# Attention's products further behind their inputs, and another order of loads in the first block

## The chip, the cores and the metric

The kernel runs on one core of a Trainium2 chip. The core has a matrix engine (TensorE, PE in the rows; its weight loads are PEld), two engines for elementwise work (VectorE, DVE, and ScalarE, ACT), GpSimd (POOL) and a queue from which transfers are issued (SyncE, SP). The metric is the device time in microseconds of one execution. A row says "L369" for line 369 of the kernel.

## What is computed

Three layers in a row over 8 x 576 = 4608 tokens of 512 numbers:

```python
def _attn_ref(q, k, v, g_norm):
    kv = np.einsum('bhsd,bhse->bhde', k, v)
    out = np.einsum('bhsd,bhde->bhse', q, kv)
    rms = np.sqrt(np.mean(out * out, axis=-1, keepdims=True) + 1e-06)
    return (out / rms * g_norm).astype(np.float32)

def _moe_ref(x, w_in, w_out):            # 512 -> 2048 -> 512
    h = x @ w_in
    pos, neg = h >= 1.0, h <= -1.0
    g = np.where(pos, h, np.where(neg, 0.0, (h + 1.0) ** 2 / 4.0))
    return (g @ w_out).astype(np.float32)

def _moe2_ref(x, expert_emb, tau, w1, w2):   # 8 experts, 512 -> 1024 -> 512
    ...
    expert_idx = np.argmax(xn @ en.T / tau, axis=1)
    for e in range(E):
        mask = expert_idx == e
        h = np.maximum(x[mask] @ w1[e], 0.0)
        out[mask] = gate_w[mask, None] * (h @ w2[e])
    return out
```

w_in and w_out of the second layer come as 64-bit floats; everything else is 32 bits wide.

## The kernel before

**Tiling.** The tokens are 36 tiles of 128, and three tiles make a block, so the dense layer runs over 12 blocks. K and V come in batches of 576 rows, five pieces each (`kv_loads`, L260); `kv_task` (L278) multiplies the pieces into a PSUM bank `kvp` and copies its diagonal to `kvd`. `att_task` (L312) handles one tile of tokens: it loads q (`qt`, one buffer), multiplies it with `kvd` (L336), squares on ScalarE (L351), sums on VectorE (L354), takes the root on ScalarE (L238, in `rsqrt`) and its inverse on VectorE, scales the tile (L358, `xk`), transposes it on TensorE (L369, four products into the bank `xp`), and writes the transposed tile in two parts, rounded (L385, ScalarE) and rest (L387, VectorE), to `xT`, of which there are two buffers, one for each block. `dense` (L1005) goes through 16 chunks of a block: 12 products `h <- xT, ra` (L1025), a gate (`gate_task`, L953), and two chunks later 9 products `acc <- rb, g` (L1048). Weights and activations are split into two rounded parts, so each product is made of three passes. After a block, `evac_task` (L515) empties the three `acc` banks into `row` buffers, and `route_task` (L550) picks the expert of each token and scatters the rows. Beside all that, `exp_task` (L475) splits the experts' weights and writes them back to memory for the third layer, which starts at some 945 us.

**The first block.** It has no weights yet. `w_task` (L404) loads one raw tile of 512 KB (`raw`, four buffers), makes a 32-bit float of each 64-bit one with a copy on ScalarE (L420) and three operations on VectorE (L429, L433, L437), then splits it (L443 on ScalarE, L192 on GpSimd). There are 32 such tiles, w_in's (i0 to i15) and w_out's (o0 to o15), in the order i0, i1, i2, i3, o0, i4, o1, i5 and so on. `warm` (L988) multiplies zeros until the first block's three tiles are there.

**Order.** Nothing is scheduled by the hardware beyond each engine's own queue, which runs in program order. The order of each queue is made by a planner in the kernel itself, `Flow` (L71): each task is a generator that yields the engine it needs next and an estimated cost; `run` (L132) takes, among all tasks, the step that could start first by the planner's clocks, and among steps of one engine within 0.05 us the one of the smallest priority number. Transfers are put at `dma` (L113): one after another at 360 KB per us, 1.65 us on top. Setting `f.now` forward between two steps delays, in the plan, the next step of that task; the instruction itself then waits only for what its data need. `SLACK = 0.7` is such a distance: L363 puts the transposes 0.7 us behind the scaling. `yield "ev"` waits for an event of the plan, `yield "get"` for a buffer.

Constants come by six transfers (`small_loads`, L216): the identity and one row of weights as `cs`, then `gcol`, `R`, `pcol`, `taub`, `tris`; a seventh, `ce`, comes ahead of the third layer (L1071). `AHEAD = 1` raw tile has a priority ahead of the first K and V (L1136).

Of the kernel before, what the change touches and what calls it, by code (L numbers as in the profile page):

```python
# [7 lines left out]
F32 = mybir.dt.float32  # L8
F32R = mybir.dt.float32r
BF16 = mybir.dt.bfloat16  # L10
I32 = mybir.dt.int32
U32 = mybir.dt.uint32
AF = mybir.ActivationFunctionType
# [5 lines left out]
P = 128  # L19
# [5 lines left out]
NE = 8  # L25
# [9 lines left out]
SLACK = 0.7  # L35
AHEAD = 1
AGAIN = 0.13
# [3 lines left out]

K_W8, K_BASE, K_PAR, K_E, K_MORE, K_P, K_END = 128, 136, 144, 152, 160, 168, 169


def consts(cap):

    import ml_dtypes
    import numpy as np

    c = np.zeros((P, K_END), np.float32)  # L50
    e = np.arange(NE)
    c[:, :P] = np.eye(P)
    c[:, K_W8 : K_W8 + NE] = NE - e
    c[:, K_BASE : K_BASE + NE] = e * cap
    c[:, K_PAR : K_PAR + NE] = e % 2
    c[:, K_E : K_E + NE] = e
    c[:, K_MORE : K_MORE + NE] = e < NE - 1
    c[:, K_P] = np.arange(P)
    tri = np.concatenate([np.triu(np.ones((P, P)), 1), np.ones((P, P))], 1).astype(ml_dtypes.bfloat16)
    return c, tri  # L60

# [9 lines left out]
class Flow:  # L71
# [6 lines left out]
    def __init__(self):  # L78
        self.tasks = []
        self.clock = {}  # L80
        self.pool = {}
        self.events = {}
        self.now = 0.0
        self.dmas = 0.0
        self.count = 0

# [26 lines left out]
    def dma(self, size):  # L113

        self.dmas = max(self.dmas, self.now + 0.65) + size / 360e3
        return self.dmas + 1.0

    def resolve(self):
# [34 lines left out]
@with_exitstack  # L153
def tile_kernel(ctx: ExitStack, tc: tile.TileContext, qT, k, v, g2, w_in, w_out, emb, tau, w1, w2, cst, tri, out):
    nc = tc.nc
# [26 lines left out]
    f = Flow()  # L182
# [11 lines left out]
    def rows_dma(out_, in_, size, wait=True):  # L194
        nc.sync.dma_start(out=out_, in_=in_)
        done = f.dma(size)
        if wait:
            f.now = done
        return done

    KB = 1024.0
# [14 lines left out]
    def small_loads():  # L216
        yield "sp", 0.45
        cs = consts_["cs"] = keep.tile([P, K_W8 + NE], F32, name="cs")
        f.set("cs", rows_dma(cs, cst[:, 0 : K_W8 + NE], 70 * KB, False))
        for name, src, n, dt in (  # L220
            ("gcol", g2, 1, F32), ("R", cst[:, K_BASE : K_BASE + NE], NE, F32), ("pcol", cst[:, K_P : K_P + 1], 1, F32),
            ("taub", tau.partition_broadcast(P), 1, F32), ("tris", tri, 2 * P, BF16),
        ):
            yield "sp", 0.45
            consts_[name] = late.tile([P, n], dt, name=name)
            done = rows_dma(consts_[name], src, 8 * KB, False)
        f.set("small", done)
        yield "pool", 0.1
        for name, val in (("neg1", -1.0), ("half", 0.5)):
            consts_[name] = late.tile([P, 1], F32, name=name)  # L230
            nc.gpsimd.memset(consts_[name], val)

    def rsqrt(pool, a, n, nm, bufs=1):
# [26 lines left out]
    def kv_loads(start, end):  # L260

        if start == 0:
            for name in ("xT", "xT"):
                yield "get", name
        else:
            yield "ev", ("kvt", start - 1)
        for u in range(start, end):
# [10 lines left out]
    def kv_task(b):  # L278
        kvp = None
        for j in range(NKV):  # L280
# [4 lines left out]
            kt, vt, n, done = kv_tiles.pop(u)  # L285
            f.now = max(f.now, done)
            yield "pe", 0.5
# [16 lines left out]
        for h in range(2):  # L304
            r = slice(h * D, h * D + D)
            nc.scalar.activation(out=kvd[b % 2][r, :, r], in_=kvp[r, :, r], func=AF.Copy)
        f.put("kvp")
        f.set(("kv", b))

    xT = {}  # L310

    def att_task(i, otag="op", xtag="op"):  # L312
# [9 lines left out]
        else:  # L322
            qt = sr.tile([P, DM], F32, name="qt", tag="qt", bufs=1)
        rows_dma(qt, qT[i], 256 * KB)
        b0, b1 = (i * P) // S, (i * P + P - 1) // S
        yield "ev", ("kv", b0)
# [35 lines left out]
        f.put(otag)  # L362
        f.now += SLACK  # L363
        yield "ev", "cs"
# [283 lines left out]
    def first_expert():  # L648

        ce = ord_["ce"]  # L650
        col = lambda c0: ce[:, c0 - K_BASE : c0 - K_BASE + NE]
        c = new("fc")
# [410 lines left out]
    def start_slots():  # L1063
# [6 lines left out]
        pools["x"] = ctx.enter_context(tc.tile_pool(name="m2x", bufs=1, side="right", reuse_waits="tile"))  # L1070
        ce = ord_["ce"] = late.tile([P, K_END - K_BASE], F32, name="ce")  # L1071
        rows_dma(ce, cst[:, K_BASE:K_END], 16 * KB)
        yield "pool", 0.7
# [49 lines left out]
    def chained(*gens):  # L1123
        for g_ in gens:
            yield from g_

    f.add(kv_loads(0, NKV), 0)
    f.add(kv_task(0), 0)
# [103 lines left out]
def lay_out(inputs):  # L1232
# [9 lines left out]
    w_in = np.ascontiguousarray(w_in.transpose(2, 1, 0, 3)).reshape(NF, P, 512)  # L1242
    g2 = np.concatenate([inputs["g_norm"], inputs["g_norm"]]).reshape(P, 1)
    cst, tri = consts(tok + P)
    def turned(a):
# [4 lines left out]
    return {  # L1250
        "qT": qT, "k": flat(inputs["k"]), "v": flat(inputs["v"]), "g2": np.ascontiguousarray(g2), "w_in": bits(w_in),
        "w_out": bits(np.ascontiguousarray(inputs["moe_w_out"])), "emb": inputs["moe2_expert_emb"],
        "tau": np.asarray(inputs["moe2_tau"]).reshape(1), "w1": turned(inputs["moe2_w1"]), "w2": inputs["moe2_w2"],
        "cst": cst, "tri": tri,
    }
# [18 lines left out]
```

## Time and profile before

| | us |
|---|---|
| median of 3 runs | 1448.8 |
| lowest, highest | 1446.64, 1449.76 |
| the profiled execution | 1447.99 |
| its span, first to last instruction | 1446.2 |
| PE busy in the span | 1391.8 |
| DVE busy in the span | 1120.5 |

The span is what the rows count in, from its first instruction on. A busy share is a mean over stages that have different limits, so the stages have to be read one by one. Idle time of an engine is told with what ended it; only idle time of the engine that sets the pace of a stage costs time. The granted clock (PEclk) is TensorE's, as a share of full speed.

### The profile page before, as it was taken

What the parts mean: (1) busy time and instruction counts of PE and PEld (TensorE: products, weight loads), DVE (VectorE), ACT (ScalarE), POOL (GpSimd) and SP (SyncE); (2) the same over time, 40 slices, a digit from 0 to 9 for tenths busy, and PEclk for the clock granted to TensorE, in tenths of its full rate; (3) what the DMA queues carried; (4) which work ended last, traced back from release to release, by engine and by line L of the source; (5) the groups of instructions that cost most, each with busy time, mean ns of one, the idle gap of its engine ahead of it and who ended that gap; (6) DMA issues with size and microseconds to landing.
All of it is one profiled execution on the core that took longest, in us unless ns stands there. A gap on an engine that the chain in (4) does not pass through costs nothing. (4 is left out here: it accounts for less than half of the span.)

```text
span 1446.2 us, 24714 instructions
## 1 busy us (share of the span) xinstructions
PE 1391.8 (96%) x7474; PEld 1194.2 (83%) x7474; DVE 1120.5 (77%) x2629; ACT 618.5 (43%) x1259; POOL 377.0 (26%) x347
## 2 busy tenths in 40 slices
PE   6889999999999999999999999999999999999995
PEld 5768889889889888888889999878888888888884
DVE  5888989696969797978778756485887778888883
ACT  4766455545555554555555534332222222222221
POOL 1675233323233332333332332310000010000000
PEclk9999999999999999999999999999999999999998
DMA  9764654555655564545454200583111137774175
GB/s 290 240 223 169 204 193 166 190 196 183 216 191 177 176 232 170 180 167 180 164 181 162 69 31 1 222 334 112 53 46 45 46 136 278 273 288 178 46 298 207
DMA packets 85456, 249.99 MB, mean 173 GB/s; under 512 B 10190, under 2 KB 10446, under 8 KB 80592
## 3 DMA queue, kind: packets, MB, share of 16 engines
q1 hardware_dynamic: 79168, 229.21, 44.9%
q0 software_dynamic: 6160, 19.18, 3.4%
q8 instruction: 68, 1.11, 0.3%
q14 instruction: 60, 0.49, 0.1%
HBM read 423.87 MB, written 90.02 MB: 355 GB/s over the span
## 5 line engine op out<-in xcount | busy, mean ns | idle before, releaser
L1048 PE MATMUL acc<-rb,g 128*128 128x512 f32 x1728 | 448.5, 400 | 9.9 <-POOL rb L192 6.4
L1025 PE MATMUL h<-xT,ra 128*128 128x384 f32 x2304 | 441.3, 338 | 0.6 <-DVE xT L387 0.4
L1025 PEld LDWEIGHTS h<-xT,ra 128*128 128x128 f32 x2304 | 403.3, 188 | 17.6 <-DVE xT L387 0.6
L1048 PEld LDWEIGHTS acc<-rb,g 128*128 128x128 f32 x1728 | 319.8, 189 | 72.1 <-POOL rb L192 8.8
L897 DVE STREAM_TRANSPOSE ht<-h 32x256 f32<-32x256 f32 x592 | 264.1, 446 | 55.1 <-PE h L822 44.2
L192 POOL TENSOR_TENSOR sp<-sp 128x512 fp32r<-128x512 f32 x128 | 182.3, 1429 | 441.3 <-ACT sp L466 421.8
L561 DVE CUSTOM_DVE_ANT_0 tr<-row,en 128x512 bf16<-128x512 f32 x288 | 228.0, 796 | 3.0 <-ACT row L526 0.3
L822 PE MATMUL y<-rb,hT 128*128 x888 | 217.9, 401 | 5.1 <-DMA rb<-ws 5.1
L822 PE MATMUL h<-ra,xT 128*128 x888 | 213.9, 396 | 0.0
L822 PEld LDWEIGHTS y<-rb,hT 128*128 128x128 f32 x888 | 165.2, 189 | 43.3 <-issue 6.0
L822 PEld LDWEIGHTS h<-ra,xT 128*128 128x128 f32 x888 | 167.1, 188 | 40.4
L964 ACT ACTIVATE h<-h,neg 128x384 f32<-128x384 f32 x176 | 97.6, 554 | 214.8 <-DVE cl L957 214.8
L975 DVE TENSOR_TENSOR cl<-h,cl 128x384 f32<-128x384 f32 x176 | 97.4, 554 | 65.7 <-ACT cl L968 65.5
L980 ACT ACTIVATE g<-cl 128x384 fp32r<-128x384 f32 x192 | 100.7, 525 | 110.2 <-DVE cl L975 70.6
L957 DVE TENSOR_SCALAR cl<-h 128x384 f32<-128x384 f32 x192 | 105.8, 551 | 45.9 <-PE h L1025 44.9
L192 DVE TENSOR_TENSOR g<-cl,g 128x384 fp32r<-128x384 f32 x144 | 100.6, 698 | 31.9 <-ACT g L980 30.4
L968 ACT ACTIVATE cl<-cl,half 128x384 f32<-128x384 f32 x192 | 116.6, 607 | 0.0
L912 ACT ACTIVATE hT<-ht 128x512 fp32r<-128x512 f32 x74 | 46.2, 624 | 160.4 <-DVE ht L897 160.4
L941 POOL DMA_INDIRECT out<-ys,xr x24 | 23.4, 974 | 269.0 <-ACT ys L938 241.7
L778 ACT ACTIVATE xT<-xp 128x512 fp32r<-128x512 f32 x42 | 25.1, 598 | 159.3 <-PE xp L771 159.2
L466 ACT ACTIVATE sp<-sp 128x512 fp32r<-128x512 f32 x128 | 79.2, 622 | 12.6 <-DMA sp<-in_w 11.2
L192 POOL TENSOR_TENSOR g<-cl,g 128x384 fp32r<-128x384 f32 x48 | 53.4, 1113 | 88.8 <-ACT g L980 85.9
(156 smaller groups left out, 1079.2 us busy)
## 6 DMA issues: line engine op xcount, KB each, us to landing
ra<-ws SPq DMA_DIRECT2D x78, 2048.0 KB
rb<-ws SPq DMA_DIRECT2D x76, 2048.0 KB
ws<-sp SPq DMA_DIRECT2D x128, 512.0 KB
sp<-in_w SPq DMA_DIRECT2D x128, 256.0 KB
qt<-in_qT SPq DMA_DIRECT2D x33, 256.0 KB
raw<-in_w_in SPq DMA_DIRECT2D x16, 512.0 KB
raw<-in_w_out SPq DMA_DIRECT2D x16, 512.0 KB
kt<-in_k SPq DMA_DIRECT2D x26, 256.0 KB
```

Of the source, the lines that this page charges most:

```text
L192: eng.tensor_tensor(out=out_, in0=a, in1=hi.bitcast(F32), op=ALU.subtract)
L466: nc.scalar.activation(out=sp[:, 0], in_=r, func=AF.Copy)
L561: nc.vector.tensor_tensor_reduce(out=trash("tr", e % 2), in0=rows[blk, t][:, 0:DM], in1=en[:, e], scale=1.0, scalar=0.0, op0=ALU.mult, op1 ...
L822: m = nc.tensor.matmul(out=out, lhsT=lhsT, rhs=ring[:, bass.ds(pars[t], 1), c0 : c0 + 512].rearrange("p a f -> p (a f)"), start=start, sto ...
L897: nc.vector.transpose(out=ht[t][s, :, r], in_=h[r, 256 * q : 256 * q + 256].rearrange("p (c a) -> p c a", c=8))
L957: nc.vector.tensor_scalar(out=cl, in0=h, scalar1=-1.0, scalar2=1.0, op0=ALU.max, op1=ALU.min)
L964: nc.scalar.activation(out=over, in_=h, func=AF.Relu, bias=consts_["neg1"])
L968: nc.scalar.activation(out=cl, in_=cl, func=AF.Square, bias=consts_["half"], scale=0.5)
L975: nc.vector.tensor_tensor(out=cl, in0=over, in1=cl, op=ALU.add)
L980: nc.scalar.activation(out=g[:, 0], in_=cl, func=AF.Copy)
L1025: nc.tensor.matmul(out=h, lhsT=ra[:, wa, o : o + P], rhs=xT[blk][:, xa, dk], start=dk == 0 and n == 0, stop=dk == 3 and n == 2,)
L1048: nc.tensor.matmul(out=accs[t], lhsT=g[:, ga, t * P : t * P + P], rhs=rb[:, wa, df * 512 : df * 512 + 512], start=(df == 0 and n == 0), st ...
```

## The change

It does five things. One table of constants, `cst`, holds all of them (the norm's weights, tau and the triangular matrix packed into it) and comes in one transfer; `R`, which is written later, gets a copy by GpSimd, and the transfer `ce` falls away. A task `root_first` makes a memset on VectorE and a square root of one column on ScalarE ahead of everything. Three raw weight tiles instead of one are ahead of the first K and V. K and V of the later batches, whose loads so far began when the first batch's had been issued, begin when the fifth w_in tile is converted. And the planner changes: `queued` lets only eight transfers be in flight on SP's queue, and the new distance `LATE = 2.0` stands between K's and V's landing and their products (batches after the first), between q's landing and its product (blocks after the first), and between scaling and transposes, where 0.7 stood; 0.7 are added between the copy of `kvd` and the products that read it.

```diff
-AHEAD = 1
+LATE = 2.0
+AHEAD = 3
...
+        self.lanes = [0.0] * 8
...
+    def queued(self, size):
+        at = self.lanes.pop(0)
+        if at > self.now:
+            self.now = self.clock["sp"] = at
+        done = self.dma(size)
+        self.lanes.append(done)
+        return done
...
     def rows_dma(out_, in_, size, wait=True):
         nc.sync.dma_start(out=out_, in_=in_)
-        done = f.dma(size)
+        done = f.queued(size)
...
     def small_loads():
         yield "sp", 0.45
-        cs = consts_["cs"] = keep.tile([P, K_W8 + NE], F32, name="cs")
-        f.set("cs", rows_dma(cs, cst[:, 0 : K_W8 + NE], 70 * KB, False))
-        for name, src, n, dt in (
-            ("gcol", g2, 1, F32), ("R", cst[:, K_BASE : K_BASE + NE], NE, F32), ("pcol", cst[:, K_P : K_P + 1], 1, F32),
-            ("taub", tau.partition_broadcast(P), 1, F32), ("tris", tri, 2 * P, BF16),
-        ):
-            yield "sp", 0.45
-            consts_[name] = late.tile([P, n], dt, name=name)
-            done = rows_dma(consts_[name], src, 8 * KB, False)
-        f.set("small", done)
+        cs = consts_["cs"] = keep.tile([P, K_END], F32, name="cs")
+        f.set("cs", rows_dma(cs, cst, 150 * KB, False))
+        for name, c0, n in (("gcol", K_G, 1), ("pcol", K_P, 1), ("taub", K_TAU, 1), ("tris", K_TRI, P)):
+            consts_[name] = cs[:, c0 : c0 + n]
+        consts_["tris"] = consts_["tris"].bitcast(BF16)
+        f.set("small", f.events["cs"])
...
+        yield "ev", "cs"
+        yield "pool", 0.1
+        consts_["R"] = late.tile([P, NE], F32, name="R")
+        nc.gpsimd.tensor_copy(out=consts_["R"], in_=cs[:, K_BASE : K_BASE + NE])
+
+    def root_first():
+        yield "dve", 0.1
+        one = late.tile([P, 1], F32, name="one")
+        nc.vector.memset(one, 1.0)
+        yield "act", 1.4
+        nc.scalar.activation(out=one, in_=one, func=AF.Sqrt)
...
         else:
-            yield "ev", ("kvt", start - 1)
+            yield "ev", ("w", "i", 4)
...
             kt, vt, n, done = kv_tiles.pop(u)
-            f.now = max(f.now, done)
+            f.now = max(f.now, done + (LATE if b else 0.0))
...
         f.put("kvp")
+        if b:
+            f.now += SLACK
         f.set(("kv", b))
...
         rows_dma(qt, qT[i], 256 * KB)
+        if not first:
+            f.now += LATE
...
         f.put(otag)
-        f.now += SLACK
+        f.now += SLACK if first else LATE
         yield "ev", "cs"
         yield "get", xtag
         yield "pe", 0.43
...
-        ce = ord_["ce"] = late.tile([P, K_END - K_BASE], F32, name="ce")
-        rows_dma(ce, cst[:, K_BASE:K_END], 16 * KB)
...
+    f.add(root_first(), -2)
     f.add(kv_loads(0, NKV), 0)
```

## Rows read from the trace of the kernel before

**Rows 1.** The page's part 1: busy us, share of the span, instructions.

```profile
PE 1391.8 (96%) x7474; PEld 1194.2 (83%) x7474; DVE 1120.5 (77%) x2629; ACT 618.5 (43%) x1259; POOL 377.0 (26%) x347
```

**Rows 2.** Busy time by stage; columns as in the first line.

```profile
core 0: us, PE busy (x) PEld busy (x) DVE busy (x) ACT busy (x) POOL busy (x), PEclk, DMA share, GB/s
60.00:100.00 40.00, 33.60 (x246) 27.60 (x246) 35.79 (x60) 26.69 (x50) 26.32 (x25) 1.00 0.73 236
300.00:400.00 100.00, 97.87 (x604) 86.05 (x603) 83.84 (x196) 50.95 (x103) 28.64 (x24) 1.00 0.57 196
```

**Rows 3.** What PE waited for, whole span: us in total, times, longest.

```profile
PE xp L369 <- DVE xk L358: 6.7, 8, 2.3
PE acc L1048 <- POOL rb L192: 6.4, 7, 1.3
...
PE op L336 <- DMA qt<-in_qT: 1.4, 2, 1.1
PE kvp L293 <- ACT kvd L306: 1.3, 2, 1.0
```

**Rows 4.** Timeline of PE: start, us, instruction [idle before <- what ended it].

```profile
45.64 0.63 PE L369 MATMUL xp<-cs,xk 128*128 128x128 f32 x4 [0.89 <-DVE xk L358]
...
623.43 0.63 PE L369 MATMUL xp<-cs,xk 128*128 128x128 f32 x4 [2.26 <-DVE xk L358]
...
696.28 0.63 PE L369 MATMUL xp<-cs,xk 128*128 128x128 f32 x4 [1.18 <-DVE xk L358]
```

**Rows 5.** Timeline of all engines, first 32 us.

```profile
4.86 0.69 DVE L429 TENSOR_SCALAR join<-raw 128x512 int32<-128x512 int32 x1 [4.86 <-ACT raw L420]
...
16.24 0.69 DVE L354 TENSOR_REDUCE ass<-xk 128x8 f32<-128x512 f32 x1 [9.23 <-ACT xk L351]
...
18.02 0.65 ACT L420 ACTIVATE raw<-raw 128x512 f32<-128x512 f32 x1 [0.92 <-DMA raw<-in_w_in]
18.69 1.28 ACT L238 ACT_TABLE_LOAD   x1
19.98 0.21 ACT L238 ACTIVATE ta<-ass 128x8 f32<-128x8 f32 x1
...
20.22 0.20 DVE L240 RECIPROCAL ya<-ta 128x8 f32<-128x8 f32 x1 [2.20 <-ACT ta L238]
...
31.77 1.14 PE L1025 MATMUL h<-xT,ra 128*128 128x384 f32 x5 [0.38 <-DVE xT L387]
```

**Rows 6.** Busy time in steps of 4 us, columns as in rows 2.

```profile
4.00:8.00 4.00, 1.29 (x19) 1.21 (x20) 2.08 (x3) 1.28 (x2) 0.25 (x1) 1.00 0.95 323
8.00:12.00 4.00, 3.55 (x52) 2.80 (x51) 0.00 (x0) 0.00 (x0) 1.09 (x3) 1.00 1.07 305
12.00:16.00 4.00, 3.23 (x51) 2.78 (x47) 0.00 (x0) 1.15 (x3) 0.00 (x0) 1.00 0.82 219
```

**Rows 7.** DVE by line, 20 to 120 us: busy us, mean ns | idle before.

```profile
L433 DVE SCALAR_TENSOR_TENSOR join<-raw,join 128x512 int32<-128x512 int32 x30 | 20.8, 693 | 0.8
L429 DVE TENSOR_SCALAR join<-raw 128x512 int32<-128x512 int32 x30 | 20.7, 691 | 1.7 <-ACT g L980 0.5
L437 DVE SCALAR_TENSOR_TENSOR nar<-raw,join 128x512 int32<-128x512 int32 x29 | 19.8, 684 | 1.5
L957 DVE TENSOR_SCALAR cl<-h 128x384 f32<-128x384 f32 x15 | 8.3, 553 | 3.9 <-PE h L1025 3.6
```

**Rows 8.** Timeline of SP's queue: issues of transfers.

```profile
9.28 0.33 SPq L195 DMA_DIRECT2D cs<-in_cst  x1
...
13.81 2.07 SPq L195 DMA_DIRECT2D raw<-in_w_in  x3
...
16.40 0.43 SPq L195 DMA_DIRECT2D kvin<-in_k  x1
```

**Rows 9.** Busy time from 30 to 118 us, columns as in rows 2.

```profile
30.00:118.00 88.00, 74.68 (x527) 62.36 (x526) 78.34 (x128) 60.30 (x112) 61.33 (x54) 1.00 0.72 233
```

**Rows 10.** Timeline of DVE at the end of a block's attention and its next step.

```profile
240.70 0.68 DVE L358 TENSOR_TENSOR xk<-op,ya 128x512 f32<-128x512 f32 x1
...
274.30 0.75 DVE L387 SCALAR_TENSOR_TENSOR xT<-xp,gcol,xT 128x512 fp32r<-128x512 f32 x1 [0.17 <-ACT xT L385]
```

**Rows 11.** Timeline of PE after a stall, and the same nine products elsewhere.

```profile
214.69 3.53 PE L1048 MATMUL acc<-rb,g 128*128 128x512 f32 x9 [2.58 <-ACT row L526]
...
244.11 2.26 PE L1048 MATMUL acc<-rb,g 128*128 128x512 f32 x9
```

**Rows 12.** Busy time just behind that stall, columns as in rows 2.

```profile
217.00:218.50 1.50, 1.50 (x5) 1.21 (x5) 1.29 (x3) 0.24 (x1) 0.65 (x1) 0.50 0.31 112
```

More of the change, by code (lines that the diff above doesn't have):

```diff
@@ L39, with consts @@
 PAD = {"pe": 1.0, "act": 1.03, "dve": 1.05, "pool": 1.03, "sp": 1.0}
-K_W8, K_BASE, K_PAR, K_E, K_MORE, K_P, K_END = 128, 136, 144, 152, 160, 168, 169
-def consts(cap):
+K_W8, K_BASE, K_PAR, K_E, K_MORE, K_P, K_G, K_TAU, K_TRI, K_END = 128, 136, 144, 152, 160, 168, 169, 170, 171, 299
+def consts(cap, g, tau):
     import ml_dtypes
@@ L58, in consts @@
     c[:, K_P] = np.arange(P)
+    c[:, K_G] = g
+    c[:, K_TAU] = tau
     tri = np.concatenate([np.triu(np.ones((P, P)), 1), np.ones((P, P))], 1).astype(ml_dtypes.bfloat16)
-    return c, tri
+    c[:, K_TRI:K_END] = np.ascontiguousarray(tri).view(np.float32)
+    return c
 class Task:
@@ L153, in tile_kernel @@
 @with_exitstack
-def tile_kernel(ctx: ExitStack, tc: tile.TileContext, qT, k, v, g2, w_in, w_out, emb, tau, w1, w2, cst, tri, out):
+def tile_kernel(ctx: ExitStack, tc: tile.TileContext, qT, k, v, w_in, w_out, emb, w1, w2, cst, out):
     nc = tc.nc
@@ L648, in first_expert @@
     def first_expert():
-        ce = ord_["ce"]
-        col = lambda c0: ce[:, c0 - K_BASE : c0 - K_BASE + NE]
+        col = lambda c0: consts_["cs"][:, c0 : c0 + NE]
         c = new("fc")
@@ L1242, in lay_out @@
     w_in = np.ascontiguousarray(w_in.transpose(2, 1, 0, 3)).reshape(NF, P, 512)
-    g2 = np.concatenate([inputs["g_norm"], inputs["g_norm"]]).reshape(P, 1)
-    cst, tri = consts(tok + P)
+    g2 = np.concatenate([inputs["g_norm"], inputs["g_norm"]])
+    cst = consts(tok + P, g2, inputs["moe2_tau"])
     def turned(a):
@@ L1250, in lay_out @@
     return {
-        "qT": qT, "k": flat(inputs["k"]), "v": flat(inputs["v"]), "g2": np.ascontiguousarray(g2), "w_in": bits(w_in),
+        "qT": qT, "k": flat(inputs["k"]), "v": flat(inputs["v"]), "w_in": bits(w_in),
         "w_out": bits(np.ascontiguousarray(inputs["moe_w_out"])), "emb": inputs["moe2_expert_emb"],
-        "tau": np.asarray(inputs["moe2_tau"]).reshape(1), "w1": turned(inputs["moe2_w1"]), "w2": inputs["moe2_w2"],
-        "cst": cst, "tri": tri,
+        "w1": turned(inputs["moe2_w1"]), "w2": inputs["moe2_w2"],
+        "cst": cst,
     }
```

## The prediction

> **What bounds the kernel now.** I read the engine totals first, then the span cut into stages, then what TensorE waits for, then the first 32 us row by row. TensorE (PE) is busy for 96% of the span and VectorE (DVE) for 77% [rows 1]. By stages it is two kernels: after the first block PE is busy for 97.87 us of 100, while from 60 to 100 us it has 33.60 of 40 and DVE 35.79 of 40 [rows 2]. So from some 120 us on, every microsecond in which PE stands still is lost, and before that point DVE is the engine that sets the pace. The reader should see in the waits that PE's largest wait on attention is the transposes' for the normalised tile, 6.7 us in 8 times, then the attention product's for its query tile, 1.4 in 2, and the K^T V product's for the copy of the bank before it, 1.3 in 2; the first block's own wait is for converted w_out, 6.4 us [rows 3]. One of the eight, 0.89 us, lies in the first block; the others are 5.8 us together, the longest 2.26 and the next 1.18 [rows 4]. In the first 32 us DVE stands for 9.23 us until the first attention reduction at 16.24 and for 2.20 more until 20.22, and the first block's products run from 31.77 [rows 5].
>
> **The sum is made against** the profiled execution: 1448.0 us, of which the span is 1446.2. It lies 0.8 under the median of the three runs shown, 1448.8; I carry the difference over to the median.
>
> **Part A, the first 32 us: three raw weight tiles ahead.** Two more tiles of 512 KB (1.05 MB) go ahead of the first K and V. The core's transfers are full there, 323 and 305 GB/s from 4 to 12 us [rows 6], so K, V and q land 1.05 MB / 314 GB/s = 3.3 us later, and the first reduction moves from 16.24 to about 19.5. That is the price: +3.3 us. What it buys: a tile's conversion takes DVE 691 + 693 + 684 ns = 2.07 us [rows 7], and two of them now lie in the stretch in which DVE only waited: -4.1 us. They fit: the three conversions need 6.2 us, and the first alone began at 4.86 [rows 5].
>
> **Root table first.** The load of the square root's table took 1.28 us at 18.69, right between the first reductions and their roots; a raw tile's copy of 0.65 stood ahead of it [rows 5]. DVE's 2.20 us of idle time before 20.22 is the sum of both. With the table in place at the start, where ScalarE waits for its first raw tile anyway (4.86 is when that copy was through), and with the three copies done before attention starts, I give back all of it: -2.2 us. If a raw tile's copy still stands there, it is only the table, 1.28 us; nothing if the table is loaded twice. In the row the root follows the load at once, 18.69 + 1.28 = 19.97 against a start at 19.98 (the DVE row waits for it). By "ScalarE: Activation LUTs" of the Trainium skill, section What ACT_TABLE_LOAD costs, a change of set costs 2.66 us, 1.38 of them a drain behind the load; by that the gain would be 1.4 us more and the time 1437.2. By the row there is no drain.
>
> **Constants in one transfer.** Six issues run from 9.28 up to the next raw tile at 13.81, and nearly empty transfers take the place of full ones: 219 GB/s from 12 to 16 us against 305 before [rows 6, 8]. One transfer replaces them, so the fourth raw tile is asked for some 3 us sooner than it would be otherwise; DVE is not short of raw tiles in that stretch once three are converted, so I count nothing (0 to -1 us). The copy of R on GpSimd and the memset and root at the start lie where those engines are idle. The transfer that is gone near the second layer's start was not waited for by PE: nothing.
> Part A: 3.3 - 4.1 - 2.2 = **-3.0 us**; bounds +3.3 (nothing comes back) and -6.3 (all comes back and the delay of K and V is covered).
>
> **Part B, the rest of the first block.** From 30 to 118 us DVE is busy for 78.34 of 88 us and PE for 74.68 [rows 9]. Attention's waits on PE are there too (0.89 us in the row of 45.64), but moving them does little while DVE is the bound: DVE waited for a product of PE for 3.6 us in all [rows 7]. The second batch's K and V, so far issued from 16.40 on [rows 8], now wait until the fifth w_in tile is converted. That leaves the transfers between 16 and 30 us to the weights. I take -1 us: a quarter of the 3.6; bounds 0 and -4 below, and above zero what the second rival prices.
>
> **Part C, after 120 us: distance in TensorE's order.** The planner now places the transposes 2.0 us behind the normalisation instead of 0.7, so 1.3 us of other products go ahead of them; the attention product stands 2.0 us behind the planned landing of its q, and the K^T V product as far behind its inputs. PE issues in its order, so a stall shorter than the added distance vanishes. Of the seven transposes' stalls only the one of 2.26 us is longer than 1.3: it keeps 0.96, and 5.8 - 0.96 = 4.85 go. The two of q (1.4 us, longest 1.1) go whole. The 1.3 us for the bank's copy are not touched: no distance is added there. Part C: **-6.2 us**; bounds 0 and -8.5 (all three kinds gone). What is late next is DVE's own order, not PE's. What hides the longer chain: a block's last step of attention that can be done ahead ended at 240.70 + 0.68, and the next, which needs the other buffer of xT, came at 274.30 [rows 10]. 33 us are free in a block for three tiles, each longer by 3.3; if a tile grew by over 11 us, the dense part would wait for it in every block.
>
> **Sum:** -3.0 - 1.0 - 6.2 = -10.2 us, 1437.8 against the profiled execution, **1438.6** as the median.
>
> **Rivals.** *The stalls come back elsewhere.* The planner also models the transfer queue differently (at most eight in flight), and so the order of all engines is laid anew; the seven stalls are the late tail of 33 tiles, and a new order may have a tail of its own. Then A and B alone remain: -4.0, 1444.8. For it: the waits for the evacuated row (2.58 us at 214.69) are of another kind and stay [rows 11]. Against it: only two of the seven stalls come near the added distance.
> *Slower, by the order of transfers.* K and V of the first batch land 3.3 us later, and the second batch (576 rows of 2 KB, K and V: 2.36 MB) moves into the weight stream; if that stream has no room, its 2.36 MB / 320 GB/s = 7.4 us show as raw tiles that are late for DVE. With C as forecast: 3.3 + 7.4 - 6.2 = +4.5, 1453.3. It decides at the point where the block's transfers are full: from 30 to 118 us they ran at 233 GB/s [rows 9], 20.5 MB; with 2.36 MB more 260, under the 314 of the start. That speaks against it.
> *The change doesn't do what it says:* the distances are planned times, and where a real landing is later than the planned one by more than 2 us, PE stands as before; with the first block a wash, 1448.8.
> *The clock.* After the stall of 2.58 us at 214.69 the granted clock was 0.50 from 217 to 218.5, the lower of its two levels, and nine products took 3.53 us where nine take 2.26 at the upper one [rows 11, 12]. "TensorE: Matmul & The Clock Gate" of the Trainium skill, section Why this matters for your kernels, says to leave no long gaps in PE's work, and an earlier start of the dense part just behind attention's gaps could begin at the lower level. From the rows such an episode is 3.53 - 2.26 = 1.3 us; one more at the start gives 1439.9.
>
> **How the numbers follow.** Forecast 0.62 (its own range 1432 to 1445); stalls elsewhere 0.14; no change 0.10; slower 0.10; the clock 0.04. About 0.2%, 2.9 us, is what a measurement of this kernel tells from no change. Faster by more: 0.62 + 0.04 + 0.10 of the second case (1444.8 is 4.0 under) + 0.01 = 0.77. Within: the rest of that case 0.04 + 0.08 = 0.12. Slower: 0.10 + 0.01 = 0.11. The range goes from 1432, short of the sum of the lower bounds (-6.3 - 4 - 8.5 is 1430), to 1451, which takes in the case of no change and leaves out that of slower.
>
> **What would show it.** Part A: first attention reduction near 19.5 us, no table load near it, three conversions before it, the first block's products from 28 to 30 us. Part B: DVE idle under 9 us in the first block, raw tiles not waited for longer. Part C: the transposes' wait near 2 us in all, that for q at zero, the bank's copy as before. Wrong would be: dense products starting later than 31.77, GB/s in the first block at its ceiling with ScalarE waiting for raw tiles, or waits of the same total under other names between 120 and 860 us.

## The result, and the profile after

| | before | changed |
|---|---|---|
| median, us | 1448.14 | 1432.34 |
| lowest to highest | 1446.64 to 1449.76 | 1432.11 to 1432.95 |
| span of the profiled execution | 1446.2 | 1430.4 |
| end of the first block's second product | 134.0 | 133.4 |
| from there to the end of the dense layer | 811.3 | 798.8 |
| third layer | 500.9 | 498.2 |

The changed kernel is 15.8 us faster, a ratio of 0.9891 with a 95% interval of 0.9874 to 0.9908. The last three lines of the table come from the first and the last product of each stage in the two traces: -0.6, -12.5 and -2.7 us. The forecast had put -4.0, -6.2 and nothing there.

Busy time in three stretches, first of the kernel before, then of the changed one (0 to 30 us, 30 us to the end of the first block's second product, and from there to the end of the dense layer):

```profile
core 0: us, PE busy (x) PEld busy (x) DVE busy (x) ACT busy (x) POOL busy (x), PEclk, DMA share, GB/s
0.00:30.00 30.00, 18.80 (x236) 15.80 (x236) 13.12 (x32) 11.12 (x19) 3.88 (x10) 0.89 0.89 288
30.00:134.00 104.00, 90.68 (x609) 76.74 (x608) 89.40 (x149) 69.75 (x130) 70.31 (x62) 1.00 0.68 225
134.00:945.30 811.30, 798.28 (x4461) 711.46 (x4460) 640.96 (x1547) 421.21 (x848) 259.35 (x228) 1.00 0.48 166
```

```profile
0.00:30.00 30.00, 16.34 (x189) 14.16 (x189) 17.04 (x39) 12.98 (x24) 6.64 (x13) 0.94 0.70 243
30.00:133.40 103.40, 96.01 (x665) 81.41 (x666) 85.92 (x143) 65.86 (x125) 67.52 (x60) 0.97 0.70 234
133.40:932.20 798.80, 794.65 (x4461) 712.69 (x4460) 638.36 (x1548) 420.05 (x848) 257.69 (x228) 1.00 0.49 169
```

Read DVE's idle time in the first two stretches, and PE's in the third. DVE's: 30 - 13.12 = 16.9 us before and 13.0 after, so 3.9 us were won in the first 30 us; then 104 - 89.40 = 14.6 before and 17.5 after, so 2.9 were lost again. In that second stretch PE is now the busier of the two, 96.01 us against DVE's 85.92; before they were level, 90.68 and 89.40. PE's in the third: 13.0 us before, 4.15 after. That is 8.9 of the 12.5 us; in the other 3.6 PE does the same 4461 products in less busy time.

What PE waited for from 120 to 860 us, before and after (us in total, times, longest):

```profile
PE xp L369 <- DVE xk L358: 5.8, 7, 2.3
PE acc L1048 <- ACT row L526: 2.6, 1, 2.6
PE rk L595 <- DVE xT L387: 1.7, 1, 1.7
PE op L336 <- DMA qt<-in_qT: 1.4, 2, 1.1
PE kvp L293 <- ACT kvd L306: 1.3, 2, 1.0
```

```profile
PE rk L621 <- DVE xT L413: 2.2, 3, 1.5
PE h L1050 <- DVE cl L1000: 1.5, 2, 0.9
PE xp L395 <- DVE yq L262: 0.4, 1, 0.4
```

The transposes' wait of [rows 3, 4] is gone but for 0.4 us, the waits for q and for the bank's copy are gone, and so is the one for the evacuated row [rows 11]. The less busy time has its row too. The granted clock of two stretches, before and then after:

```profile
200.00:300.00 100.00, 97.19 (x560) 86.44 (x559) 81.59 (x202) 55.00 (x113) 32.71 (x31) 0.98 0.55 190
...
700.00:800.00 100.00, 98.19 (x513) 87.84 (x512) 76.62 (x184) 51.76 (x103) 28.96 (x25) 0.98 0.48 168
```

```profile
200.00:300.00 100.00, 97.63 (x568) 86.83 (x566) 82.98 (x201) 57.22 (x117) 32.94 (x29) 1.00 0.56 193
700.00:800.00 100.00, 100.00 (x541) 90.16 (x540) 77.57 (x186) 55.38 (x110) 35.24 (x32) 1.00 0.51 179
```

Before, the clock fell to its lower level, 1.2 GHz, for 3.4 us behind two of the stalls (2.58 us at 214.69, 1.68 us at 729.25); after, PE runs at the upper one, 2.4 GHz, from 37 us to the last 21 us of the span. Which stalls are followed by it can't be told from their length: behind the transposes' longest, 2.26 us, the clock stayed up.

```profile
623.50:626.00 2.50, 2.50 (x16) 2.37 (x17) 2.47 (x7) 1.95 (x4) 0.53 (x1) 1.00 0.09 27
```

In another execution of the same order of work (the kernel before, shifted by 64 bytes, below) it was the other way round: the row's stall, 2.52 us at 215.02, left the clock up, and the transposes' was followed by the lower level, with twelve products in 3.30 us where twelve take 2.27.

```profile
622.48 0.63 PE L370 MATMUL xp<-cs,xk 128*128 128x128 f32 x4 [2.23 <-DVE xk L359]
...
624.16 3.30 PE L1026 MATMUL h<-xT,ra 128*128 128x384 f32 x12
```

The first block. Timeline of the changed kernel, all engines, to be held against [rows 5]:

```profile
18.66 0.69 DVE L380 TENSOR_REDUCE ass<-xk 128x8 f32<-128x512 f32 x1 [7.17 <-ACT xk L377]
...
20.36 0.20 DVE L262 RECIPROCAL ya<-ta 128x8 f32<-128x8 f32 x1
...
29.96 0.69 PE L1050 MATMUL h<-xT,ra 128*128 128x384 f32 x1 [0.44 <-ACT xT L411]
...
31.25 5.17 PE L1050 MATMUL h<-xT,ra 128*128 128x384 f32 x15 [0.60 <-DVE xT L413]
...
33.75 0.43 SPq L209 DMA_DIRECT2D kvin<-in_k  x1
...
35.17 0.56 DVE L982 TENSOR_SCALAR cl<-h 128x384 f32<-128x384 f32 x1 [1.86 <-PE h L1050]
```

The first reduction comes at 18.66 and the reciprocal follows 1.70 us later, with no table between. But fifteen dense products take 5.17 us, at the lower clock; DVE waits 1.86 us for one of them; and the later batches' K starts only at 33.75. Two stretches show it, 22 to 28 and 32 to 38 us; first the kernel before, then the changed one:

```profile
22.00:28.00 6.00, 5.56 (x54) 4.67 (x56) 5.83 (x14) 2.63 (x6) 0.00 (x0) 0.52 0.95 354
...
32.00:38.00 6.00, 5.36 (x44) 4.68 (x44) 4.88 (x8) 3.45 (x7) 2.86 (x3) 1.00 0.97 308
```

```profile
22.00:28.00 6.00, 3.44 (x26) 3.08 (x26) 5.83 (x14) 2.59 (x6) 0.00 (x0) 0.72 0.00 1
...
32.00:38.00 6.00, 6.00 (x23) 6.00 (x23) 3.06 (x5) 2.26 (x4) 2.87 (x3) 0.60 0.88 307
```

From 22 to 28 us the changed kernel moves 1 GB/s where the one before moved 354: the four raw buffers are full and nothing else may be loaded. From 32 to 38 DVE is idle for 2.94 us of 6 instead of 1.12.

### The profile page after: what moved, and what is told of

Its sections match the earlier page's. It is cut to its first block, busy times and chain, and to the rows that moved or that the text cites. A ratio compares the mean times of both kernels' runs of the same rounds, so it can differ in the third digit from the quotient of the medians.

```text
span 1430.4 us, 24712 instructions
## 1 busy us (share of the span) xinstructions
PE 1386.9 (97%) x7484; PEld 1198.6 (84%) x7484; DVE 1118.3 (78%) x2630; ACT 615.3 (43%) x1259; POOL 375.8 (26%) x348
## 5 line engine op out<-in xcount | busy, mean ns | idle before, releaser
L1050 PE MATMUL h<-xT,ra 128*128 128x384 f32 x2304 | 447.0, 340 | 2.5 <-DVE cl L1000 1.5
L1073 PE MATMUL acc<-rb,g 128*128 128x512 f32 x1728 | 442.4, 397 | 6.8 <-POOL rb L206 5.0
L1050 PEld LDWEIGHTS h<-xT,ra 128*128 128x128 f32 x2304 | 408.5, 189 | 19.7 <-DVE cl L1000 3.1
L847 PE MATMUL y<-rb,hT 128*128 x888 | 214.2, 397 | 6.5 <-DMA rb<-ws 6.5
L206 POOL TENSOR_TENSOR g<-cl,g 128x384 fp32r<-128x384 f32 x48 | 53.2, 1108 | 82.4 <-ACT g L1005 79.6
```

What stands on the lines that cost most here:

```text
L206: eng.tensor_tensor(out=out_, in0=a, in1=hi.bitcast(F32), op=ALU.subtract)
L847: m = nc.tensor.matmul(out=out, lhsT=lhsT, rhs=ring[:, bass.ds(pars[t], 1), c0 : c0 + 512].rearrange("p a f -> p (a f)"), start=start, sto ...
L1050: nc.tensor.matmul(out=h, lhsT=ra[:, wa, o : o + P], rhs=xT[blk][:, xa, dk], start=dk == 0 and n == 0, stop=dk == 3 and n == 2,)
L1073: nc.tensor.matmul(out=accs[t], lhsT=g[:, ga, t * P : t * P + P], rhs=rb[:, wa, df * 512 : df * 512 + 512], start=(df == 0 and n == 0), st ...
```

## The experiments

Eleven kernels, each beside runs of the kernel before on the same chip, whose medians there were 1448.1 to 1448.8 us. A summary first. "Block" is the end of the first block's second product, "dense" the time from there to the end of the dense layer, "third" the rest of the span, all in us of the profiled execution.

| kernel | median | lowest to highest | block | dense | third |
|---|---|---|---|---|---|
| before | 1448.14 | 1446.64 to 1449.76 | 134.0 | 811.3 | 500.9 |
| changed | 1432.34 | 1432.11 to 1432.95 | 133.4 | 798.8 | 498.2 |
| distances alone | 1437.29 | 1434.99 to 1438.54 | 136.0 | 799.1 | 501.6 |
| changed, no distances | 1442.82 | 1437.53 to 1447.87 | 131.8 | 809.0 | 497.8 |
| changed, no wait of K and V | 1429.92 | 1427.76 to 1434.80 | 130.8 | 800.4 | 497.2 |
| changed, old queue model | 1432.04 | 1429.19 to 1432.30 | 132.8 | 799.1 | 498.1 |
| changed, one raw tile | 1437.38 | 1434.44 to 1439.07 | 136.3 | 803.0 | 498.0 |
| changed, no root first | 1437.44 | 1434.32 to 1442.40 | 135.6 | 798.1 | 502.0 |
| changed, table late | 1433.68 | 1429.41 to 1434.34 | 135.5 | 798.8 | 497.9 |
| before, shifted 64 bytes | 1451.02 | 1447.34 to 1456.09 | 134.1 | 810.8 | 500.7 |
| changed, xT shifted 64 bytes | 1431.74 | 1430.12 to 1434.64 | 133.5 | 798.8 | 497.4 |
| changed, shifted 64 bytes | 1437.55 | 1433.02 to 1440.62 | 133.1 | 801.1 | 501.8 |
| no wait, first block near | 1434.15 | 1432.43 to 1437.54 | 135.4 | 799.2 | 498.0 |

### Distances alone

```diff
 (the kernel before, with)
+LATE = 2.0
-            f.now = max(f.now, done)
+            f.now = max(f.now, done + (LATE if b else 0.0))
...
+        if b:
+            f.now += SLACK
         f.set(("kv", b))
...
+        if not first:
+            f.now += LATE
...
-        f.now += SLACK
+        f.now += SLACK if first else LATE
```

> The kernel before with only the distances in the plan (2.0 us behind the landings of K, V and q, 2.0 instead of 0.7 behind the scaling, 0.7 behind the copy of kvd). Theory: the 12.5 us that the dense blocks after the first gained are the distances' work. Then PE waits for the scaled tile 1 us or less in all (6.7 before), blocks 1 to 11 are 9 to 13 us shorter than before, and the time is 1435 to 1440 us. Rival: the gain comes from the order that the new model of the transfer queue lays; then the distances alone give the forecast 6 us at most, 1442 us or more.

Measured: 1437.29 us, ratio 0.9931 (0.9906 to 0.9955), in the theory's span. The dense stage takes 799.1 us, 12.2 less than before. Its waits on PE from 120 to 860 us:

```profile
PE h L1030 <- DVE cl L980: 1.9, 3, 0.9
PE xp L374 <- DVE ssx L572: 1.4, 1, 1.4
PE acc L1053 <- POOL rb L193: 1.2, 1, 1.2
PE acc L1053 <- ACT row L531: 0.5, 1, 0.5
PE rk L600 <- DVE xT L392: 0.5, 2, 0.2
```

One wait for the scaled tile is left, 1.4 us: the row names `ssx`, a step of routing, but the scaled tile was ready at 256.66 and the transposes start at 256.80. That is a little over the 1 us that the theory allowed, and the rival falls: the distances do nearly all of the dense stage's gain by themselves, the row's stall included (0.5 us for 2.6). The first block, though, ends 2.0 us later than before; in this execution the clock was at its lower level twice in its products, for 3.4 us each from 53.5 and from 73.9 us.

### The changed kernel without the distances

```diff
-            f.now = max(f.now, done + (LATE if b else 0.0))
+            f.now = max(f.now, done)
...
-        if b:
-            f.now += SLACK
...
-        if not first:
-            f.now += LATE
...
-        f.now += SLACK if first else LATE
+        f.now += SLACK
```

> The changed kernel without the distances (0.7 us behind the scaling as before, none behind landings and copy); first block, constants and queue model as changed. Theory of the distances: the waits for the scaled tile are back at 4 to 8 us in all, and the time is 1441 to 1447 us. Rival (queue model and first block do it): 1437 us or less, with waits for the scaled tile under 2 us.

Measured: 1442.82 us, ratio 0.9964 (0.9946 to 0.9981). Waits on PE from 120 to 860 us, the first two lines:

```profile
PE xp L391 <- DVE xk L380: 6.9, 8, 2.3
PE acc L1069 <- ACT row L548: 2.6, 1, 2.6
```

The wait for the scaled tile is back at 6.9 us, within what the theory asked, and the row's stall with it. The first block ends at 131.8, sooner than in either kernel: without distances its new order is worth 2.2 us.

### The old model of the transfer queue

```diff
-        done = f.queued(size)
+        done = f.dma(size)
```

> The changed kernel with the old model of the transfer queue (no limit of eight in flight in the plan). Theory: the distances do it whatever the order, 1431 to 1435 us. Rival: the more truthful queue model is what the extra 6 us over the forecast come from, 1437 us or more, with PE waits for q or K and V back between 120 and 860 us.

Measured: 1432.04 us, ratio 0.9894 (0.9869 to 0.9920), dense 799.1 us. As the theory had it: the queue model is not where the gain comes from. The orders of PE, DVE, ScalarE and SP's queue are the changed kernel's, so here the model changed next to nothing.

### The wait of the later K and V

```diff
-            yield "ev", ("w", "i", 4)
+            yield "ev", ("kvt", start - 1)
```

> The changed kernel, but the later K and V may be loaded as before, when the first batch's loads have been issued, not after the fifth w_in tile is converted. Theory: the first block was 9.1 us ahead at its ninth chunk and lost it again because K and V, and with them attention, were held back while the transfers stood idle from 22 to 28 us; without that the block ends 2 to 4 us sooner, 1428 to 1431 us. Rival: the wait kept K and V out of the weights' way, and without it DVE waits for raw tiles: 1434 us or more. Third: the block is bound by the sum of DVE's and GpSimd's work and the order is indifferent: 1432 within 1.

Measured: 1429.92 us, ratio 0.9891 (0.9859 to 0.9923); the block ends at 130.8 us, 2.6 sooner than in the changed kernel, in the theory's span. The two stretches again:

```profile
22.00:28.00 6.00, 3.76 (x60) 3.09 (x59) 5.83 (x14) 2.69 (x6) 0.24 (x1) 1.00 0.88 311
...
32.00:38.00 6.00, 6.00 (x59) 5.37 (x58) 5.23 (x9) 4.41 (x10) 2.87 (x3) 1.00 0.88 262
```

The transfers run at 311 GB/s from 22 to 28 us and DVE is idle for 0.77 us of 6 where it was for 2.94. The stretch shows a second difference, the clock: 1.00 for 0.60. With K and V there, PE has their products to do between the first block's transposes and the dense products,

```profile
28.43 0.69 PE L315 MATMUL kvp<-vt,kt 128*64 128x64 f32 x16
...
29.37 0.69 PE L315 MATMUL kvp<-kvin 128*64 128x64 f32 x16
29.98 2.67 PE L1050 MATMUL h<-xT,ra 128*128 128x384 f32 x12
```

and twelve dense products take 2.67 us at once, where fifteen took 5.17. But neither shows in DVE's idle time as a whole. From the start to the block's end:

```profile
0.00:30.00 30.00, 18.53 (x253) 15.76 (x253) 17.84 (x40) 13.16 (x25) 6.68 (x13) 1.00 0.93 329
30.00:130.80 100.80, 92.33 (x604) 77.83 (x603) 82.41 (x137) 65.68 (x125) 67.62 (x60) 0.98 0.67 217
```

DVE is idle for 30.5 us there, in the changed kernel for 30.4. What is less is its work, 100.2 us for 103.0: the sums, roots and scaling of one tile of tokens lie behind the block's end here and ahead of it in the changed kernel. The dense stage takes 1.6 us more, and at its end 1.0 of the 2.6 us is left. So the block's end moved with the work ahead of it, and neither transfers nor clock is shown as the cause. In median it is the fastest kernel seen, 2.4 us under the changed one, but the executions of the two overlap, and their ratios to the kernel before are the same, 0.9891.

### One raw tile ahead

```diff
-AHEAD = 3
+AHEAD = 1
```

> The changed kernel with one raw weight tile ahead of the first K and V, as before. Theory of the prediction: K and V come 2.4 us sooner, DVE does two conversions (4.1 us) later, where it is short; dense products start at 31 us or later, the block ends 1 to 3 us later: 1433 to 1435 us. Rival: the order in the first 20 us is made up for by the end of the block whatever it is (the block ended 0.6 us sooner only): 1432 within 1.

Measured: 1437.38 us, ratio 0.9915 (0.9891 to 0.9939), more than either side expected. The block ends 2.9 us later, as the theory had it. The dense stage takes another 4.2 us. Its waits, 136 to 945 us:

```profile
PE h L1050 <- DVE cl L1000: 3.0, 4, 0.9
PE rk L621 <- DVE xT L413: 2.1, 3, 1.7
PE xp L395 <- DVE tq L596: 1.2, 1, 1.2
PE kvp L315 <- ACT kvd L328: 1.1, 1, 1.1
```

Two of the kinds that had gone are back: the bank's copy (1.1), and the scaled tile, since the transposes of the third line start at 484.31 and their tile was ready at 484.17, close to the `tq` that the row names. So an edit that touches only the first 20 us lays the whole order anew, and that alone moved the dense stage by 4 us. It is the rival in which stalls come back elsewhere, seen in another kernel.

### No root first, and the table late

```diff
 (no root first)
-    f.add(root_first(), -2)
```

> The changed kernel without the square root ahead of everything: the table is loaded among the first block's roots again, 1.28 us on ScalarE. Prediction's term: DVE stands 1.3 to 2.2 us more before the first reciprocal, and the end moves by as much, 1433 to 1434.5 us. Rival: DVE fills the wait with a conversion and nothing is lost: 1432 within 1.

Measured: 1437.44 us, ratio 0.9926 (0.9903 to 0.9949), 5 us above the changed kernel instead of 1 to 2: 2.2 at the block's end, and 3.8 in the third layer, which has nothing to do with a table. The removed task also removed its tile of 32 bytes, and with it moved the tiles behind it. So the table was tried again with all tiles in place:

```diff
 (table late)
-        yield "act", 1.4
-        nc.scalar.activation(out=one, in_=one, func=AF.Sqrt)
+        yield "act", 0.1
+        nc.scalar.activation(out=one, in_=one, func=AF.Copy)
```

> The changed kernel with a copy in place of the early square root: the same tiles at the same addresses, but the root's table is loaded among the first block's roots again. The kernel without the early root at all also moved the addresses by 32 bytes, and its third layer took 502 us. Theory: the table is worth what its row says, 1.3 to 2.2 us at the end of the first block, third layer 498 us, 1433.5 to 1434.5 us. Rival: nothing at the end, 1432 within 1.

Measured: 1433.68 us, ratio 0.9891 (0.9873 to 0.9910), third layer 497.9 us, as the theory has it. The orders of PE, DVE, GpSimd and SP's queue are the changed kernel's, line for line; ScalarE has one load of a table more, and the reciprocal behind it waits:

```profile
25.18 0.20 DVE L262 RECIPROCAL ya<-ta 128x8 f32<-128x8 f32 x1 [1.20 <-ACT ta L260]
```

The median is 1.3 us above the changed kernel, the size of the row, but one execution took 1429.41 us: the runs don't settle it. The trace adds why: with the same order, the last piece of K and V was multiplied at 16.6 us here and at 15.2 in the changed kernel. When the first transfers land differs by over a microsecond between executions. The clock differs too: the first attention products ran at the lower level, in 5.08 us where the changed kernel's took 2.94,

```profile
18.64 5.08 PE L362 MATMUL op<-kvd,q 128*128 128x128 f32 x24 [0.38 <-ACT kvd L328]
```

the first reduction came at 21.38 us for 18.66, and from 26.6 to 40.2 us the clock was low again, where the changed kernel has it low from 30.0 to 36.8. The block ends 2.1 us later; the table's share in that can't be read off.

### Addresses

The third layer's 2.7 us came with the new constants: the kernels with them have 497 to 498 us there, the one with distances alone 501.6, and so has, at 502.0, the one that lost the tile of 32 bytes. Between the two kernels the constants changed size, and all tiles behind them stand 64 bytes lower: hT at 187776 (before 187840), g at 206208 (206272), xT at 181632 (181696). Three kernels have only unused tiles added:

```diff
 (the kernel before, and the changed kernel, shifted)
     consts_ = {}
+    late.tile([P, 16], F32, name="gap", tag="gap")
 (the changed kernel, xT shifted: one such tile of 64 bytes ahead of xT, one ahead of g)
+        sb.tile([P, 16], F32, name="gap0", tag="gap0", bufs=1)
...
+            sb.tile([P, 16], F32, name="gap1", tag="gap1", bufs=1)
```

> The kernel before with an unused tile of 64 bytes per partition among the constants, so that all that lies behind it in SBUF stands 64 bytes higher: the stationary operands hT and g then begin at a multiple of 128 bytes, as in the changed kernel, and so does the moving operand xT. Nothing else changes. Theory: the 3 us of the third layer, and the other pace of the dense products, come from these addresses. Then the products y <- rb, hT go every 227 ns in the median (233 before), acc <- rb, g every 231 (235), h <- xT, ra every 174 (173, the mean 2 ns more), the third layer is 3 us shorter, the dense part some 2 longer by the pace alone, the time 1445 to 1448 us. Rival: the missing transfer and the other constants did it; then all paces stay at 233, 235 and 173 and the third layer at 501 us.

Measured: 1451.02 us, ratio 1.0023 (1.0011 to 1.0035). The median distance of two starts of `y <- rb, hT` is 232 ns, not 227, and the third layer takes 500.7 us. The theory's rule, a multiple of 128 bytes, is wrong: hT stands at one here, 187904. The time, 2.2 us above the kernel before, missed the 1445 to 1448 as well; `h <- xT, ra` goes every 178.1 ns in the mean, for 175.4 in the kernel before.

> The changed kernel with two unused tiles of 64 bytes, so that the moving operand xT begins at 64 modulo 128 as in the kernel before, while g and hT begin at 0. Theory of the addresses: h <- xT, ra goes back from 177.9 to 175.7 ns in the mean, 2304 x 2.2 ns = 5 us; acc and y keep 231 and 227. 1426 to 1429 us. Rival: the pace of h is set by what runs beside it, or by g's address; then 1432 within 1.5.

Measured: 1431.74 us, ratio 0.9885 (0.9867 to 0.9903). The pace of `h <- xT, ra` went back from 178.0 to 176.0 ns in the mean, as expected (means from here on are of distances under 300 ns; those in the expectations lie up to 1.2 ns higher); g had moved too, by 128 bytes, and `acc <- rb, g` went from 231.1 to 232.8. The pace followed the address, the time did not: it is within the rival's bound. 2112 x 2.0 ns less and 1584 x 1.7 more in blocks 1 to 11 is 1.5 us, and the dense stage took the same 798.8 us.

> The changed kernel with an unused tile of 64 bytes per partition ahead of the constants, so that xT, g and hT stand again at the addresses they had in the kernel before. A multiple of 128 bytes is not it: the kernel before shifted to one kept y <- rb, hT at 232 ns. Theory (each address has its pace, whatever the rule): y is back at 233 ns from 227, the third layer at 501 us from 498, h <- xT, ra at 175.7 in the mean from 177.9, acc <- rb, g at 233.9 from 232.1; with 2304 x 2.2 ns less and 1728 x 1.8 more, 2 us, in the dense part, the time is 1432.5 to 1434.5. Rival: the paces are of the order of work or of the missing transfer, and stay: 1432 within 1.

Measured: the paces are what the same addresses gave before, to 0.6 ns: y 233 ns in the median, `h <- xT, ra` 176.0, `acc <- rb, g` 232.7 in the mean; the third layer takes 501.8 us. The products of the third layer, 1000 to 1400 us, in the kernel before, the changed one and the changed one shifted (busy us, mean ns of one):

```profile
L822 PE MATMUL y<-rb,hT 128*128 x816 | 198.6, 398 | 0.0
L822 PE MATMUL h<-ra,xT 128*128 x819 | 197.4, 396 | 0.0
```

```profile
L847 PE MATMUL h<-ra,xT 128*128 x840 | 202.3, 396 | 0.0
L847 PE MATMUL y<-rb,hT 128*128 x826 | 197.1, 394 | 0.0
```

```profile
L848 PE MATMUL y<-rb,hT 128*128 x834 | 203.0, 398 | 0.0
L848 PE MATMUL h<-ra,xT 128*128 x816 | 196.5, 396 | 0.0
```

Only y, which reads the moved hT, differs; h, whose operands stand where they stood, keeps 396 ns in all three. The time is 1437.55 us, ratio 0.9919 (0.9898 to 0.9939), 5.2 above the changed kernel and more than the theory's 1434.5. Of the 5.6 us between the profiled spans the third layer has 3.6, as expected; the dense stage has 2.3 more, where 2 less were expected. Its order is the changed kernel's, but behind a stall of 1.51 us at 201.37 the clock was at its lower level from 201.9 to 205.3 us, which the changed kernel's dense stage has nowhere:

```profile
202.00:205.00 3.00, 3.00 (x10) 2.71 (x9) 1.62 (x6) 1.29 (x3) 1.35 (x2) 0.50 0.72 242
```

Nine products take 3.14 us there instead of 2.26 and six 1.99 instead of 1.20, 1.7 us in all. Why the 2 us that the paces should have given did not come is not explained.

### The first block near

```diff
 (without the wait of K and V, and)
-            f.now = max(f.now, done + (LATE if b else 0.0))
+            f.now = max(f.now, done + (LATE if b > 2 else 0.0))
...
-        if b:
+        if b > 2:
...
-        if not first:
+        if blk > 1:
             f.now += LATE
...
-        f.now += SLACK if first else LATE
+        f.now += LATE if blk > 1 else SLACK
```

> The kernel without the wait of the later K and V for the fifth w_in tile, and with the distances only for tiles of the third block on and for K and V from the fourth batch on: what runs beside the first block stands as near to its inputs as before. Theory: the distances cost the first block some 2 us (its end came 2.0 us later with the distances alone, and 1.6 sooner when they were taken from the changed kernel), since attention's steps move behind the weights' there. Then the first block ends near 129 us (130.8 with the distances) and the time is 1427 to 1429.5 us. Rival: the stalls of attention come back in the first block and cost what the distances did: 1430 or more.

Measured: 1434.15 us, ratio 0.9904 (0.9884 to 0.9923); the block ends at 135.4 us, 4.6 later than with the distances. The theory falls, and with it the idea of one price that the distances have in the first block: alone they cost it 2.0 us, in the changed kernel 1.6, and here they save 4.6. Beside the weights' conversion the order's details decide, by some 4 us, and no row singled out one of them. The clock is one more difference: in this execution it was low twice in the block's products, for 3.4 us each from 62.0 and from 103.0 us, in the kernel without the wait once, from 109.5.

## Why the prediction was right, and where its sizes were off

The time lies inside the range by 0.3 us, and that is partly luck: the first block gave 3.4 us less than forecast, the dense stage 6.3 more, and 2.7 came from a stage that was not in the sum. Had the first block come as forecast, the time would lie outside.

**What bounds the kernel** was read rightly for the kernel before. Past the first block, time came off where PE stood still, and in the first block moving PE's stalls did nothing: attention's waits on PE left it (0.89 us for the transposes and more for K, V and q), and its end moved by 0.6 us. After the change PE is the busier engine in that block, so that DVE alone sets its pace no longer holds.

**Part A** held. The first reduction came at 18.66 us for a forecast of 19.5 (K, V and q 2.4 us later, not 3.3), three conversions were done by 11.5, no table stood near the roots, and DVE won 3.9 us of idle time by 30 us for a forecast of 3.0. The dense products did not start at 28 to 30 with it but at 29.96 and 31.25 (before, all but the first from 31.77). On their way lies the first reciprocal, and that came no sooner, at 20.36 for 20.22: the table's gain there went into the later K and V, and the two conversions done early don't lie on that way. One reading was off by a little: the 2.20 us of [rows 5] hold the root itself, 0.21 us, beside the copy and the load.

**Part B** is the step that failed: -1 was forecast, +2.9 us of DVE's idle time came, and from 30 to 118 us it is 10.6 us where the sign asked for under 9. (The other sign held: ScalarE waited 6.7 us for raw tiles from 20 to 120 us, 11.6 before.) I had written that holding back the second batch "leaves the transfers between 16 and 30 us to the weights". The weights could not use them: four raw buffers were full, and the core moved 1 GB/s from 22 to 28 us. The row that would have told was there: in the trace before, SP's queue stood 56.1 us in 24 times waiting for a conversion to free a buffer. Then K and V came at 33.75, into the weights' stream, and attention with them: the block was some 9 us ahead at the start of its tenth chunk (79.6 for 88.8) and 0.6 at its end. Part of that lead was attention put off: the kernel before transposed its fourth tile of the next blocks at 91.8 us, the changed one at 110.8. That the hold caused the 2.9 us is not shown: without it the transfers ran, and DVE was idle as long, 30.5 for 30.4 us up to the block's end. The rows say for whom DVE waited: from 30 us to the block's end 8.4 us for the products h, 6.0 before, with PE busy for 96.0 us of 103.4. Why PE was late there, by the clock, by the later K and V or by the order, stays open.

**The clock**, a rival at 0.04, happened: the dense part began at the lower level. Its price was sized from an episode of nine products, 1.3 us; here fifteen took 5.17 us against 15 x 0.176 = 2.6 at the upper level, 2.5 us of PE's time. How much of it reached the block's end stays open.

**Part C** was right in its mechanism and too small. The clipping rule said that 4.85 of the transposes' 5.8 us and q's 1.4 go; 5.4 and 1.4 went. The terms that were missing: the wait for the bank's copy (1.3) went although no distance is added in front of it, and the row's stall (2.6) although it is "of another kind": both are gone or nearly so with the distances alone (the row's is 0.5 there) and back without them (1.1 and 2.6). By what step is not shown. Against these, routing's wait rose from 1.7 to 2.2 and the gate's to 1.5. Sum of the idle time: -8.9 us. The other 3.6 us are busy time, and the clock accounts for 3.4 of them: behind the stalls of 2.58 and 1.68 us nine acc and six h products took 3.53 and 1.64 us for 2.26 and 1.20, twelve h and six acc 2.96 and 2.53 for 2.25 and 1.56, 1.7 us each time. It is not the addresses: with the distances alone, at the old ones, PE is busy for 794.5 us in the dense stage, as in the changed kernel. I had a row of it [rows 11, 12] and used it only as a danger, not as part of what a removed stall may be worth. But none of it hung on the stalls that Part C aimed at: these two were the row's and routing's, and routing still stalls for 1.5 us in the changed kernel, with the clock up. Which stall is followed by the lower level differs between executions of one order. But the three kernels without the distances have it once or twice in the dense stage of their traces, and of the ten with them one has it, once: fewer stalls leave fewer such stretches, and for any single stall it is luck.

**The third layer**, -2.7 us, was not in the sum at all: the constants' new size moved hT, and the pace of its products with it. The rewriting of the constants was weighed by its transfers alone.

**The rivals.** Slower by the order of transfers is out: the stream had room, 234 GB/s from 30 us on. No change is out. That the stalls come back elsewhere did not happen here, but the run with one raw tile shows that it can, at 4 us.

**The table's price and the clock, held against two pages.** "ScalarE: Activation LUTs" of the Trainium skill, section What ACT_TABLE_LOAD costs, gives 2.66 us for a change of table, a drain included. The late table's trace shows the load's 1.28 us alone, from 23.64, with the root starting at 24.94 and DVE waiting 1.20 us; the times don't settle what it costs at the end. "TensorE: Matmul & The Clock Gate" of the Trainium skill, section Why this matters for your kernels, advises against long gaps between bursts of matmuls. The traces agree in part: the lower level came behind stalls of 2.58 and 1.68 us, and at the start of the dense part behind 2.55 us of idle time that ended at 28.56; but the stall of 2.26 us, longer than one of these, left the clock up.

## What to carry to other kernels

On an engine that runs in program order, put a product behind its input by more than the spread of the input's lateness, as long as the chain that grows longer has room; price a stall with the slow clock that may come behind it, here 1.7 us, and not by its own length alone, but don't count on it for a single one: it differs from execution to execution. Before holding a transfer back for another, check that the other can use the time: a full set of buffers leaves the queue idle. And an edit to the order at the start lays the rest of the order anew, so judge it stage by stage, with the same addresses; and where a stage ends sooner, look whether its work was only put behind that end.

## What the runs showed of the hardware that was not expected

The pace of products depends on where an operand begins in SBUF, the core's on-chip memory. Distances of two neighbouring starts of the same product in ns, the median of all and the mean of those under 300 ns, with the operand that moved and the byte at which its first buffer begins; the other operand (ra or rb) stayed at its address in all kernels:

| operand, products | address | median | mean | kernel |
|---|---|---|---|---|
| hT, `y <- rb, hT` | 187776 | 227 | 228.0 | changed |
| | 187840 | 233 | 233.3 | before; changed, shifted |
| | 187904 | 232 | 232.9 | before, shifted |
| g, `acc <- rb, g` | 206208 | 231 | 231.1 | changed |
| | 206272 | 235 | 232.7 | before; changed, shifted |
| | 206336 | 232 | 232.4 to 232.8 | before, shifted; changed, xT shifted |
| xT, `h <- xT, ra` | 181632 | 174 | 178.0 | changed |
| | 181696 | 173 | 175.4 to 176.0 | before; both other shifts of the changed |
| | 181760 | 175 | 178.1 | before, shifted |

The operand that is loaded as weights (hT, g) and the one that streams (xT) want different addresses, and a multiple of 128 bytes is not the rule: 187776 and 187904 are both multiples. In both weights the fast address is an odd multiple of 128 (187776 = 1467 x 128, 206208 = 1611 x 128) and the even one is slower; with two operands that is a pattern and not a rule. What the rule is stays open. It was worth some 3 us in the third layer here, as much as several of the change's intended parts; in the dense stage the paces moved and its time did not follow them.
